# Channel squares of an attention batch from twelve extra loads, and a changed number of unsplit score steps

## The chip, the cores and the metric

The kernel runs on one core of a Trainium2 chip. The metric is the device time of one execution in microseconds (us). Three runs of the kernel before took 2171.54 to 2172.01 us, with a median of 2171.8 us.

## The reference

Four batches (B = 4) of q, k and v with N = 6080 positions and C = 256 channels go through an attention over channels, and its output through a dense layer with a hidden width of 2048:

```python
def _attn_ref(q, k, v, tau):
    qn = q / (np.linalg.norm(q, axis=1, keepdims=True) + 1e-06)
    kn = k / (np.linalg.norm(k, axis=1, keepdims=True) + 1e-06)
    s = kn.transpose(0, 2, 1) @ qn / tau
    s = s - s.max(-1, keepdims=True)
    a = np.exp(s)
    a /= a.sum(-1, keepdims=True) + 1e-09
    return (v @ a).astype(np.float32)

def _moe_ref(x, w_in, w_out):
    h = x @ w_in
    g = h - np.tanh(h)
    return (g @ w_out).astype(np.float32)
```

The norms run over the 6080 positions, one for each channel of q and of k. They are needed before the softmax, but not before the product of k and q, since each is a factor of a row or a column of the scores.

## The kernel before, in words

**Per batch.** The scores are a 256x256 matrix, summed in one PSUM bank over 48 steps of 128 positions (the last has 64). The steps are loaded in groups: group 0 is one step, groups 1 to 23 two steps each, group 24 the tail. From scores and norms comes the softmax matrix e, which is transposed and multiplied into w_in (the "fold", tile `ps_w`, eight pieces of 256 hidden units). The folded weights then meet v in blocks of 2x512 positions by a scheme of seven products (tiles `x`, `y`, `z`), ScalarE (ACT) and VectorE (DVE) form h - tanh(h), and a second product (`ps_o`) gives the output. Six blocks by eight pieces are 48 rounds for each batch, and TensorE (PE) runs them one after another for most of the time.

**Two kinds of score steps.** A plain step (`score`, line 489, with `load_plain`, line 410) multiplies fp32 as it was loaded: two matmuls of 256 columns, which the profile shows as four records. A split step takes a tile `raw`, has ACT write its rounded part and DVE the rest (`split_hi`, `split_lo`, lines 475 and 482), and needs six matmuls in the shorter format. Batch 0 uses 48 plain steps. Batch 1 uses `FILLS` = 48 plain steps, that is all of them, as fillers: the planner puts them on PE where the next instruction of the main line would come late. Batches 2 and 3 use split steps between the rounds.

**Loads at the start.** SyncE (SP) issues every load, in one order, on one queue. A group of q and k is 512 KB (one step 256 KB, the tail 128 KB) and goes into whatever is free at the start: the tiles `vhl` (eight), `gh`/`gl`, `qh`, `ql`; the groups of batch 1 take `qh` and `ql` in turn, two tiles each. Between them stand the pieces of w_in and w_out (`raw_wi`, `raw_wo`, 512 KB each), their converted copies on the way back to memory (`wi_d`), and v (`vraw`, 1 MB).

**Norms of batch 0.** After PE has read a group, ACT squares it in place (`square_plain`, line 424), and DVE and GpSimd (POOL) add the squares of each step, three of four on DVE, to three accumulators (`accumulate`, line 441). At the end ACT copies two of them out of PSUM (`take_squares`), and PE sums over the partitions with matmuls against ones (`sum_squares`, line 451, tile `ps_n`). DVE turns the sums into factors (`add_squares`, `norms`, `scales`), PE spreads one of them (`ps_b`), DVE and ACT make the softmax, PE transposes it (`ps_t`), and the fold starts (`ps_w`). The norms of the other batches come from channel-major loads (`load_channels`, `square`, lines 507 and 516): there a channel is a partition, and ACT's accumulator sums the squares of a row.

**The order of the work.** Nothing is reordered on the chip: a planner (`Plan.order`, line 129) lists all operations ahead of time from costs and due times, and each engine runs its list in order. `plain_load`, `plain_step` and `plain_square` (lines 1059 to 1073) and the loop behind them enter the operations of the first phase.

Of the kernel before, what the change touches and what calls it, by code (L numbers as in the profile page):

```python
# [10 lines left out]
F32 = mybir.dt.float32  # L11
# [3 lines left out]
AF = mybir.ActivationFunctionType  # L15
ALU = mybir.AluOpType
AX = mybir.AxisListType

P = 128
GJ = 2  # L20
NMAX = 512
NSQ = 760
# [13 lines left out]
    ("p6", []), ("p2", [4, "c"]), ("p5", [2]), ("p7", [3, "a", 6]), ("p4", ["d"]), ("p1", [1]), ("p3", [4, "b", 4]),  # L36
]
EARLY = 6
FILLS = 48
FILL_EVERY = 0.6  # L40
LEAD = 6
FIRST = 3
PAD = 208
LAG = 30
# [166 lines left out]
def act_cost(n):  # L211
    return 0.14 + n * 0.0009


def dve_cost(n):
    return 0.157 + n * 0.00104
# [8 lines left out]


@with_exitstack
def attn_moe(ctx: ExitStack, tc: tile.TileContext, qk, v4, qkT, tau, w_in, w_out, outT):

# [3 lines left out]
    nc = tc.nc  # L235
    B, N, _, C = qk.shape
    KC = C // P
# [3 lines left out]
    NJ = N // P  # L241
# [3 lines left out]
    while s0 < N:  # L245
        n = min(NMAX, (N - s0) // 2)
# [10 lines left out]
    g_p = ctx.enter_context(tc.tile_pool(name="g_p", bufs=4))  # L257
# [3 lines left out]
    sm_p = ctx.enter_context(tc.tile_pool(name="sm_p", bufs=1))  # L261
    ps_p = ctx.enter_context(tc.tile_pool(name="ps_p", bufs=1, space=bass.MemoryType.PSUM))
    ring = {
        "wi": Ring(3), "f": Ring(3), "fx": Ring(1), "raw": Ring(3), "qh": Ring(2), "ql": Ring(2), "nt": Ring(2),
        "vraw": Ring(1), "vt": Ring(1), "vhl": Ring(8),
        "u": Ring(3), "c": Ring(4), "t": Ring(4), "gh": Ring(5), "gl": Ring(5), "ob": Ring(2),
    }

    def sb(pool, tag, shape, dtype, name):
        return pool.tile(list(shape), dtype, tag=tag, name=name, bufs=ring[tag].bufs)  # L270

    def bank(i, name, shape=(P, 512)):

        return ps_p.tile(list(shape), F32, tag=f"bank{i}", name=name)
# [6 lines left out]
    def products(out, terms, first, last):  # L281

        seq = []
        for (wh, wl), (xh, xl) in terms:
            seq += [(wh, xh)] if wl is None else [(wh, xl), (wh, xh), (wl, xh)]
        for i, (w, x) in enumerate(seq):
            ins = nc.tensor.matmul(  # L287
                out, w, x,
                start=first and i == 0, stop=last and i == len(seq) - 1,
                skip_group_check=True,  # L290
            )
        return ins
# [63 lines left out]
    wi = {}  # L356
# [30 lines left out]
    groups = []  # L387
    j = 0
    while j < NJ:
        n = min(GJ, NJ - j) if j else NJ % GJ or GJ  # L390
# [7 lines left out]
    class Attn:  # L398
# [117 lines left out]
        def square(self, i):  # L516
# [3 lines left out]
            row, part = divmod(i, N // NSQ)  # L520
            nc.scalar.activation(x, x, AF.Square, accum_out=self.squares[:, row, part:part + 1])

        def add_squares(self):
            self.x = sm_p.tile([P, 2 * KC], F32, name="x")
            if self.acc is None:
                nc.vector.tensor_reduce(self.x, self.squares, axis=AX.X, op=ALU.add)
                nc.vector.tensor_scalar(self.x, self.x, 1e-37, None, op0=ALU.max)
            else:
                nc.vector.tensor_scalar(self.x, self.pn[:, 0:2 * KC], 1e-37, None, op0=ALU.max)

        def norms(self):

# [74 lines left out]


        def fold(self, s, i):
            w = wi.pop((self.b, s))  # L610
            pw = self.pw[s] = bank(i, f"ps_w_{self.b}_{s}", (P, KC, FB))
            for m in range(KC):
                ms = slice(m * P, (m + 1) * P)
                products(
                    pw[:, m, :],
                    [((self.eh[:, kk, ms], self.el[:, kk, ms]), (w[:, 0, kk, :], w[:, 1, kk, :])) for kk in range(KC)],
                    first=m == 0, last=m == KC - 1,
                )
# [79 lines left out]
    plan = Plan()  # L698
# [66 lines left out]
    def banks(gs):  # L765

        return {"X": 2 * (gs % 2), "Y": 1, "Z": 2 - 2 * (gs % 2)}
# [175 lines left out]
    ats = {}  # L943
    beside = {}

    def task(gs, place, what):
        beside.setdefault((gs, place), []).append(what)

    for s in range(FIRST, NS2):
        task(s - 2, "a", lambda s=s: plan_fold(0, s, banks(s - 2)["Z"]))  # L950
# [11 lines left out]
    def plan_softmax(a, sq, ps):  # L962

        r, d, rq, e, total = Buf("r"), Buf("d"), Buf("rq"), Buf("se"), Buf("rs")
        a.ebuf = Buf("e")

        def norms():
            plan.add("DVE", 0.4, a.add_squares, reads=[sq], writes=[r])
            plan.add("DVE", 1.8, a.norms, writes=[r])
            plan.add("DVE", 0.6, a.scales, reads=[r], writes=[d])  # L970

        def spread(z):
            pb = Buf(z)
            plan.add("PE", 0.25, lambda: a.spread(z), reads=[d], writes=[pb], late=0.0 if a.b else 1.0)
            plan.add("ACT", act_cost(C), a.take_spread, reads=[pb], writes=[rq])

        def softmax():
            for m in range(KC):
                plan.add("DVE", 1.1, lambda m=m: a.scaled(m), reads=[ps, rq, r], writes=[e])
                plan.add("ACT", act_cost(C) + 0.1, lambda m=m: a.exp(m), writes=[e])  # L980
            plan.add("DVE", 0.3, a.shares, reads=[e], writes=[total])

        def transpose(z):
            pt = Buf(z)
            plan.add("PE", 0.5, lambda: a.transpose(z), reads=[e], writes=[pt], late=0.0 if a.b else 1.0)
            plan.add("ACT", act_cost(KC * C), a.take_hi, reads=[pt, total], writes=[a.ebuf])
            plan.add("DVE", dve_cost(KC * C), a.take_lo, reads=[pt], writes=[a.ebuf], port=False)

        return norms, spread, softmax, transpose
# [65 lines left out]
    held = {}  # L1055

    scored = []

    def plain_load(b, g):
        at_ = tags[g % len(tags)] if b == 0 else tags[-2 + g % 2]  # L1060
        held[b, g] = [Buf(ring[t[1]]) for t in at_]
        plan.add(
            "SP", 0.35 * len(at_), lambda: ats[b].load_plain(g, at_), writes=held[b, g], size=0.26 * groups[g][1], after=scored if b else (), due=None if b or g > 0 else -20.0 + g,
        )

    def plain_step(b, i, due=None):
# [6 lines left out]
    def plain_square(g):  # L1073
        nonlocal adds
        x = held[0, g]
        if g == 0:
            plan.add("ACT", act_cost(1024), lambda: ats[0].square_plain(g), reads=x, writes=acc)
        else:
            plan.add("ACT", act_cost(1024), lambda: ats[0].square_plain(g), writes=x)
            for j in range(groups[g][1]):  # L1080
                i = adds % 4
                adds += 1
                if i < 3:
                    plan.add(
                        "DVE", dve_cost(2 * C), lambda i=i % 2, j=j: ats[0].accumulate(nc.vector, g, j, i),
                        reads=x, writes=[acc[i % 2]], port=False,
                    )
                else:
                    plan.add(
                        "POOL", pool_cost(2 * C), lambda j=j: ats[0].accumulate(nc.gpsimd, g, j, 2), reads=x, writes=[acc[2]],  # L1090
                    )

    tau_b = Buf("tau_sb")
    plan.add("SP", 0.35, lambda: nc.sync.dma_start(tau_sb, tau), writes=[tau_b], due=0.0)
    for i, (g, jj) in enumerate(steps):
        if jj == 0 and g in early:
            plan_w_in(early[g], due=plan.pe_time, tag="wi" if early[g] < FIRST else "f")
        if i == len(steps) - LEAD:
            scored.append(plan.last_pe)
        plain_step(0, i)  # L1100
        if jj == groups[g][1] - 1:
            plain_square(g)
        if i == 8:
            pt = Buf(1)
            plan.add("PE", 0.1, spread_tau, reads=[tau_b], writes=[pt])
            plan.add("DVE", 0.2, take_tau, reads=[pt], port=False)
    after_scores = plan.pe_time

    fills = [plain_step(1, i, after_scores + FILL_EVERY * i) for i in range(FILLS)]

    sq, pn = [Buf(ring["u"]) for _ in range(2)], Buf(1)
    for x in range(2):
        plan.add("ACT", act_cost(GJ * C), lambda x=x: ats[0].take_squares(x), reads=acc[x:x + 1], writes=sq[x:x + 1])
    plan_moving(0, scored)
    plan.add("PE", 12 * 0.22, lambda: ats[0].sum_squares(1), reads=sq + acc[2:], writes=[pn], late=1.0)
    norms, spread, softmax, transpose = plan_softmax(ats[0], pn, scores[0])
    norms()
    spread(2)
# [6 lines left out]
    for s in range(NS2):  # L1125
        plan_convert(convert_w_out(s), wobuf[s], due=after_scores + 10.0 * s, alone=s > 0)
    for s in range(FIRST, NS2):
        task(max(s - 4, 0), "start", lambda s=s: plan_w_in(s, after=[plan.last_pe], alone=True) if s > EARLY else plan_load_w(0, s))
    for b in range(1, B):
# [3 lines left out]

        plan_scores(b, [(g0 + x0, x) for x0 in range(NS2 + 1 if b == 1 else first, SLOTS - 6) for x in "ab"], ps, FILLS if b == 1 else 0)
        plan_ends(b, plan_channels(b, g0 + first, g0 + SLOTS - 12), ps)
# [21 lines left out]
    for gs in range(TOTAL):  # L1157
# [3 lines left out]
        for name, then in ORDER:  # L1161
# [6 lines left out]
            for x in then:  # L1168
                if isinstance(x, int):
                    lag, x = max(0, lag - x), max(0, x - lag)  # L1170
# [48 lines left out]
```

## Time and profile before

| | |
|---|---|
| median of three runs | 2171.8 us |
| the profiled execution's own time | 2172.18 us |
| its span | 2170.4 us |
| PE busy | 2160.2 us, 10042 matmuls |
| PE weight loads busy | 1817.4 us |
| DVE busy | 1751.0 us |
| ACT busy | 1528.9 us |
| POOL busy | 37.5 us |
| moved by DMA | 342.23 MB |

The span runs from the first instruction to the end of the last one, and the execution's own time is 1.8 us more than it. Busy time is a share of the whole span, so it says little about the first 100 us, in which other work is done than later. A matmul's end is modelled, so PE counts as busy from a matmul's start to a modelled end that overlaps the next one's start; the pace of the work is read from the distance of starts.

### The profile page before, as it was taken

The page shows a single profiled execution, that of the slowest core. Times are in us where ns is not written, and L with a number is a line of the kernel's source. Part 1 is how long each engine was busy: PE and PEld are TensorE (multiplying, and loading weights), DVE is VectorE, ACT ScalarE, POOL GpSimd, SP SyncE. Part 2 cuts the span into 40 slices and gives each one's busy share as a digit, 9 for nine tenths or more (in the row PEclk, how much of TensorE's full clock was granted, in tenths as well). Part 3 has the DMA queues.
Part 4 walks back from the last instruction along what each step waited for, and adds up shares of the span by engine and source line. Part 5 has one row for each costly group of instructions (what it writes and reads, how often), then busy time and mean ns, then how long its engine had stood idle before and what let it go on. Part 6 is the DMA issues. An engine that isn't in the chain of part 4 may idle for free.

```text
span 2170.4 us, 28453 instructions
## 1 busy us (share of the span) xinstructions
PE 2160.2 (100%) x10042; PEld 1817.4 (84%) x10042; DVE 1751.0 (81%) x2842; ACT 1528.9 (70%) x2755; POOL 37.5 (2%) x33
## 2 busy tenths in 40 slices
PE   8999999999999999999999999999999999999999
PEld 7888888888888888888888888888888888888887
DVE  8889877888888777778788877877878878778776
ACT  6566778776777777776677767777667766666665
POOL 5100000000000000000000000000000000000000
PEclk9999999999999999999999999999999999999999
DMA  9944444443454444543345445354333342332331
GB/s 385 346 162 147 163 168 148 161 155 105 151 209 150 172 164 168 181 160 140 126 144 188 170 162 189 143 189 166 128 134 128 122 147 89 128 130 92 125 120 53
DMA packets 82783, 342.23 MB, mean 158 GB/s; under 512 B 9042, under 2 KB 13138, under 8 KB 80082
## 3 DMA queue, kind: packets, MB, share of 16 engines
q1 hardware_dynamic: 82642, 340.43, 43.1%
q8 instruction: 79, 1.29, 0.2%
q14 instruction: 62, 0.51, 0.1%
HBM read 281.94 MB, written 58.46 MB: 157 GB/s over the span
## 4 chain that ended last, share of the span: by engine, by line
PE 97%; DMA 3%; SPq 0%; issue 0%; DVE 0%; ACT 0%
PE ps_o L903 48%; PE x L287 24%; PE y L287 12%; PE z L287 6%; PE ps_s L287 5%; PE ps_w L287 2%; DMA gh<-qk_dram 1%; DMA ql<-qk_dram 1%; DMA vhl<-qk_dram 0%; DMA qh<-qk_dram 0%; DMA raw_wi<-w_in_dram 0%; PE ps_n L456 0%; PE ps_t L598 0%; PE ps_b L563 0%; SPq L464 0%
## 5 line engine op out<-in xcount | busy, mean ns | idle before, releaser
L287 PE MATMUL x<-v,f 128*128 128x512 f32 (+1 forms) x2304 | 613.9, 388 | 0.0
L903 PE MATMUL ps_o<-gh,wo_h 128*128 128x512 f32 (+1 forms) x1536 | 596.8, 389 | 0.0
L903 PE MATMUL ps_o<-gh,wo_l 128*128 128x512 f32 (+1 forms) x1536 | 596.3, 388 | 0.0
L843 DVE TENSOR_TENSOR gl<-t,gh 128x512 fp32r<-128x512 f32 (+1 forms) x768 | 512.4, 680 | 57.7 <-ACT gh L839 55.7
L839 ACT CAST gh<-t 128x512 fp32r<-128x512 f32 (+1 forms) x768 | 463.5, 617 | 68.4 <-DVE t L835 61.1
L287 PEld LDWEIGHTS x<-v,f 128*128 128x128 f32 x2304 | 432.5, 188 | 87.2
L903 PE MATMUL ps_o<-gl,wo_h 128*128 128x512 f32 (+1 forms) x1536 | 472.5, 388 | 0.0
L831 ACT ACTIVATE t<-c 128x512 f32<-128x512 f32 (+1 forms) x576 | 361.1, 627 | 132.6 <-DVE c L819 127.7
L835 DVE TENSOR_TENSOR t<-c,t 128x512 f32<-128x512 f32 (+1 forms) x576 | 392.0, 682 | 75.4 <-ACT t L831 67.8
L803 ACT COPY u<-x 128x512 f32<-128x512 f32 (+1 forms) x384 | 223.6, 582 | 238.5 <-PE x L287 237.4
L903 PEld LDWEIGHTS ps_o<-gh,wo_l 128*128 128x128 f32 x1536 | 288.6, 188 | 56.5 <-ACT gh L839 0.3
L903 PEld LDWEIGHTS ps_o<-gl,wo_h 128*128 128x128 f32 x1536 | 288.6, 188 | 55.3
L903 PEld LDWEIGHTS ps_o<-gh,wo_h 128*128 128x128 f32 x1536 | 288.7, 188 | 53.2
L819 DVE TENSOR_TENSOR c<-u,y 128x512 f32<-128x512 f32 (+1 forms) x384 | 260.7, 679 | 83.7 <-ACT u L803 50.1
L287 PE MATMUL y<-v,f 128*128 128x512 f32 (+1 forms) x1152 | 321.9, 388 | 0.0
L287 PEld LDWEIGHTS y<-v,f 128*128 128x128 f32 x1152 | 216.2, 188 | 43.3 <-DVE t L835 0.3
L831 ACT ACTIVATE t<-x 128x512 f32<-128x512 f32 (+1 forms) x192 | 113.7, 592 | 114.4 <-PE x L287 112.7
L835 DVE TENSOR_TENSOR t<-x,t 128x512 f32<-128x512 f32 (+1 forms) x192 | 131.3, 684 | 72.1 <-ACT t L831 70.4
L819 DVE TENSOR_TENSOR c<-p,z 128x512 f32<-128x512 f32 (+1 forms) x192 | 130.7, 681 | 69.9 <-PE z L287 65.8
L287 PE MATMUL z<-v,f 128*128 128x512 f32 (+1 forms) x576 | 161.2, 388 | 0.0
L287 PEld LDWEIGHTS z<-v,f 128*128 128x128 f32 x576 | 108.1, 188 | 21.5
L803 ACT COPY p<-x 128x512 f32<-128x512 f32 (+1 forms) x192 | 111.8, 582 | 9.6 <-PE x L287 6.7
(121 smaller groups left out, 1494.6 us busy)
## 6 DMA issues: line engine op xcount, KB each, us to landing
f<-f_d SPq DMA_DIRECT2D x160, 896.0 KB, 4.6
nt<-qkT_dram SPq DMA_DIRECT2D x96, 380.0 KB, 5.7
f_d<-f SPq DMA_DIRECT2D x32, 896.0 KB, 3.8
raw<-qk_dram SPq DMA_DIRECT2D x46, 512.0 KB, 5.5
vraw<-v_dram SPq DMA_DIRECT2D x20, 1024.0 KB, 7.8
outT_dram<-ob SPq DMA_DIRECT2D x80, 256.0 KB, 3.0
wi<-wi_d SPq DMA_DIRECT2D x28, 512.0 KB, 5.4
vhl<-qk_dram SPq DMA_DIRECT2D x14, 512.0 KB, 9.8
```

Source lines behind the costliest of these rows:

```text
L287: ins = nc.tensor.matmul(out, w, x, start=first and i == 0, stop=last and i == len(seq) - 1, skip_group_check=True,)
L803: nc.scalar.copy(self.tiles[to], self.tiles["X"][:, 0:self.n])
L819: nc.vector.tensor_add(self.tiles[i], self.tiles[u], self.tiles[ps][:, 0:self.n])
L831: nc.scalar.activation(self.tiles["t", i], self.tiles[c][:, 0:n], AF.Tanh)
L835: nc.vector.tensor_sub(x, self.tiles[c][:, 0:n], x)
L839: nc.scalar.copy(self.g[i][0], self.tiles["t", i])
L843: nc.vector.tensor_sub(self.g[i][1], self.tiles["t", i], self.g[i][0].bitcast(F32))
L903: nc.tensor.matmul(outs[key + (m,)][:, 0:n], (wo_l if part else wo_h)[:, f, m * P:(m + 1) * P], quad.g[i][x], start=first and j == 0, stop ...
```

## The change

Twelve loads are added (`load_early`): the squares of the last twelve full steps of batch 0 (groups 18 to 23) are no longer made by squaring and adding the plain tiles. Instead the host passes those positions of q and k once more, channel-major (`qkE`), in 12 pieces of 128 channels by 512 positions (256 KB each). ACT squares each with its accumulator (`square_early`), DVE adds the three sums of a channel (`add_early`), and `add_squares` adds that to the sums of the other 36 steps. `FILLS` goes from 48 to 43, so that groups 22 to 24 of batch 1 (five steps) become split steps among the rounds. The second group's load has a due time that puts it ahead of the first piece of w_in.

```diff
-FILLS = 48
+FILLS = 43
+LO = 34
+CM = 12
...
+        def load_early(self, i):
+            row, part = divmod(i, CM * P // NMAX)
+            self.channels[i] = sb(g_p, "c", [P, NMAX], F32, f"c_{self.b}_{i}")
+            nc.sync.dma_start(
+                self.channels[i], qkE[row // KC, row % KC * P:(row % KC + 1) * P, part * NMAX:(part + 1) * NMAX],
+            )
+        def square_early(self, i):
...
+            nc.scalar.activation(x, x, AF.Square, accum_out=self.squares[:, row, part:part + 1])
+        def add_early(self):
+            self.x = sm_p.tile([P, 2 * KC], F32, name="x")
+            nc.vector.tensor_reduce(self.x, self.squares[:, :, 0:CM * P // NMAX], axis=AX.X, op=ALU.add)
         def add_squares(self):
...
             else:
-                nc.vector.tensor_scalar(self.x, self.pn[:, 0:2 * KC], 1e-37, None, op0=ALU.max)
+                nc.vector.tensor_add(self.x, self.pn[:, 0:2 * KC], self.x)
+            nc.vector.tensor_scalar(self.x, self.x, 1e-37, None, op0=ALU.max)
...
-            "SP", 0.35 * len(at_), lambda: ats[b].load_plain(g, at_), ..., due=None if b or g > 0 else -20.0 + g,
+            "SP", 0.35 * len(at_), lambda: ats[b].load_plain(g, at_), ..., due=None if b or g > 1 else -20.0 + g,
...
-        if jj == groups[g][1] - 1:
+        if jj == groups[g][1] - 1 and not NJ - CM <= groups[g][0] < NJ:
             plain_square(g)
+        if LO <= i < LO + early_squares:
+            c = Buf(ring["c"])
+            n = i - LO
+            plan.add("SP", 0.35, lambda n=n: ats[0].load_early(n), writes=[c], size=0.26, due=plan.pe_time)
+            plan.add("ACT", act_cost(NMAX) + 0.1, lambda n=n: ats[0].square_early(n), reads=[c], writes=[cm])
...
     plan.add("PE", 12 * 0.22, lambda: ats[0].sum_squares(1), reads=sq + acc[2:], writes=[pn], late=1.0)
+    plan.add("DVE", 0.25, ats[0].add_early, reads=[cm], writes=[cm])
```

On SP, at the loads of the last groups of batch 0 (`vhl_0_18` to `vhl_0_24`), the list before is this; the numbers in a name are batch and group, and a last one that only counts tiles:

```order
L464 DMA vhl_0_18_325<-qk_dram 128x1024
L464 DMA vhl_0_19_332<-qk_dram 128x1024
L464 DMA vhl_0_20_341<-qk_dram 128x1024
L464 DMA vhl_0_21_348<-qk_dram 128x1024
L375 DMA wi_d3_99<-w_3_189 128x1024
L464 DMA vhl_0_22_364<-qk_dram 128x1024
L464 DMA vhl_0_23_372<-qk_dram 128x1024
L467 DMA vhl_0_24_379<-qk_dram 64x512
L322 DMA raw_wo0_387<-w_out_dram 128x1024
L322 DMA raw_wo1_395<-w_out_dram 128x1024
L464 DMA qh_1_0_411<-qk_dram 128x512
```

The same place in the change, from the seventh of the twelve new loads (`c_0_6`) on:

```order
L529 DMA c_0_6_370<-qkE_dram 128x512
L466 DMA vhl_0_20_376<-qk_dram 128x1024
L529 DMA c_0_7_381<-qkE_dram 128x512
L466 DMA vhl_0_21_384<-qk_dram 128x1024
L377 DMA wi_d3_99<-w_3_184 128x1024
L529 DMA c_0_8_401<-qkE_dram 128x512
L466 DMA vhl_0_22_405<-qk_dram 128x1024
L529 DMA c_0_9_413<-qkE_dram 128x512
L529 DMA c_0_10_420<-qkE_dram 128x512
L469 DMA vhl_0_24_425<-qk_dram 64x512
L466 DMA vhl_0_23_431<-qk_dram 128x1024
L529 DMA c_0_11_436<-qkE_dram 128x512
```

Eleven of the twelve new loads now stand ahead of the last load of batch 0, and all twelve ahead of the first load of batch 1; the piece `raw_wo1` has moved behind the loads of batch 1's group 6.

On PE, ahead of the first fold (`ps_w_0_0`), the list before has these filler steps around the transpose (`ps_t`); a full group is four matmuls here, a step two:

```order
L287 MATMUL ps_s_1_448<-ql_1_9_554 128x256 x4
L598 MATMUL ps_t_0_610<-ident_82,s_567 128x128 x4
L287 MATMUL ps_s_1_448<-qh_1_10_573 128x256 x4
L287 MATMUL ps_s_1_448<-ql_1_11_593 128x256 x4
L287 MATMUL ps_s_1_448<-qh_1_12_602 128x256 x2
L287 MATMUL ps_w_0_0_649<-wi_0_0_109,eh_620 128x256 x2
```

And in the change:

```order
L289 MATMUL ps_s_1_472<-qh_1_8_560 128x256 x4
L289 MATMUL ps_s_1_472<-ql_1_9_585 128x256 x2
L619 MATMUL ps_t_0_637<-ident_82,s_591 128x128 x4
L289 MATMUL ps_s_1_472<-ql_1_9_585 128x256 x2
L289 MATMUL ps_s_1_472<-qh_1_10_598 128x256 x4
L289 MATMUL ps_w_0_0_659<-wi_0_0_111,eh_647 128x256 x2
```

The fold stood behind 24 filler steps, and stands behind 21 of them now; 24 of 48 were left behind it before, and 22 of 43 are now.

On SP, the first five loads before:

```order
L464 DMA vhl_0_0_106<-qk_dram 128x512
L322 DMA raw_wi0_108<-w_in_dram 128x1024
L1094 DMA tau_sb_89<-tau_dram 1x1
L464 DMA vhl_0_1_112<-qk_dram 128x1024
L322 DMA raw_wi1_114<-w_in_dram 128x1024
```

And in the change:

```order
L466 DMA vhl_0_0_106<-qk_dram 128x512
L466 DMA vhl_0_1_108<-qk_dram 128x1024
L324 DMA raw_wi0_110<-w_in_dram 128x1024
L1117 DMA tau_sb_89<-tau_dram 1x1
L324 DMA raw_wi1_114<-w_in_dram 128x1024
```

Group 1 and the first piece of w_in have changed places; what follows is the same.

## Rows read from the trace of the kernel before

**Rows 1.** The page: span, and DMA share in 40 slices of 54 us.

```profile
span 2170.4 us, 28453 instructions
...
DMA  9944444443454444543345445354333342332331
```

**Rows 2.** Waits of PE over the whole span: us in total, times, longest.

```profile
PE ps_s L287 <- DMA vhl<-qk_dram: 5.9, 3, 3.5
PE ps_s L287 <- DMA ql<-qk_dram: 0.3, 1, 0.3
```

**Rows 3.** Chain that ended last, first 85 us: start us, us, what.

```profile
2.41 6.63 DMA raw_wi<-w_in_dram
...
9.05 9.40 DMA gh<-qk_dram
...
43.55 9.22 DMA ql<-qk_dram
...
62.66 6.07 DMA ql<-qk_dram
```

**Rows 4.** Windows: engines' busy us, granted clock, DMA share, GB/s.

```profile
10.00:20.00 10.00, 10.00 (x44) 8.44 (x43) 7.74 (x15) 6.39 (x8) 4.18 (x3) 1.00 1.03 416
20.00:30.00 10.00, 10.00 (x48) 8.80 (x47) 9.47 (x14) 8.32 (x13) 8.23 (x6) 1.00 1.04 413
30.00:40.00 10.00, 9.84 (x46) 8.31 (x45) 8.72 (x15) 7.51 (x10) 7.13 (x6) 1.00 1.03 420
40.00:50.00 10.00, 10.00 (x47) 8.79 (x47) 9.69 (x15) 6.71 (x8) 6.41 (x6) 1.00 1.03 383
50.00:60.00 10.00, 9.76 (x53) 7.94 (x52) 9.76 (x18) 4.48 (x7) 4.04 (x4) 0.95 1.03 422
...
70.00:80.00 10.00, 10.00 (x54) 8.94 (x53) 8.21 (x18) 2.37 (x7) 0.71 (x1) 1.00 0.87 283
```

**Rows 5.** Timeline of SP's issues: start us, us, what.

```profile
9.05 0.33 SPq L464 DMA_DIRECT2D gh<-qk_dram  x1
10.29 0.33 SPq L464 DMA_DIRECT2D gl<-qk_dram  x1
...
18.47 0.33 SPq L464 DMA_DIRECT2D gh<-qk_dram  x1
19.10 0.33 SPq L464 DMA_DIRECT2D gl<-qk_dram  x1
...
38.58 0.56 SPq L467 DMA_DIRECT2D vhl<-qk_dram  x1
```

**Rows 6.** DMA issues of the first 80 us: KB each, median us to landing.

```profile
vhl<-qk_dram SPq DMA_DIRECT2D x1, 128.0 KB, 10.1
```

**Rows 7.** Timeline of PE: start us, us, what, idle before and its releaser.

```profile
3.52 2.07 PE L287 MATMUL ps_s<-vhl 128*128 128x256 f32 x4 [3.52 <-DMA vhl<-qk_dram]
7.79 8.86 PE L287 MATMUL ps_s<-vhl 128*128 128x256 f32 x32 [2.20 <-DMA vhl<-qk_dram]
...
23.04 1.03 PE L287 MATMUL ps_s<-gl 128*128 128x256 f32 x4
23.90 1.03 PE L287 MATMUL ps_s<-gh 128*128 128x256 f32 x4
...
51.58 1.13 PE L287 MATMUL ps_s<-qh 128*128 128x256 f32 x4
...
56.37 0.50 PE L456 MATMUL ps_n<-ones,sq 128*128 128x1 f32 x4
...
58.97 3.66 PE L287 MATMUL ps_s<-ql 128*128 128x256 f32 x8
...
78.62 0.59 PE L287 MATMUL ps_w<-wi,eh 128*128 128x256 f32 x2
```

**Rows 8.** Timeline of DVE in the same stretch.

```profile
52.09 3.07 DVE L444 TENSOR_TENSOR acc<-vhl,acc 128x512 f32<-128x512 f32 x5
...
64.10 1.49 DVE L557 TENSOR_SCALAR diag<-ident,r 128x128 f32<-128x128 f32 x2
```

**Rows 9.** Chain at 700 us: a split step of batch 2.

```profile
702.58 0.71 PE ps_s L287 x6
```

**Rows 10.** Windows, as in rows 4: the low clock, and the rounds behind the start.

```profile
58.90:62.40 3.50, 3.50 (x10) 2.50 (x10) 3.20 (x10) 0.87 (x2) 1.27 (x1) 0.52 1.01 373
...
90.00:190.00 100.00, 100.00 (x470) 83.80 (x469) 92.47 (x167) 69.07 (x126) 0.00 (x0) 1.00 0.54 199
```

More of the change, by code (lines that the diff above doesn't have):

```diff
@@ L227, in attn_moe @@
 @with_exitstack
-def attn_moe(ctx: ExitStack, tc: tile.TileContext, qk, v4, qkT, tau, w_in, w_out, outT):
+def attn_moe(ctx: ExitStack, tc: tile.TileContext, qk, v4, qkT, qkE, tau, w_in, w_out, outT):
     nc = tc.nc
@@ L521, in square @@
             nc.scalar.activation(x, x, AF.Square, accum_out=self.squares[:, row, part:part + 1])
+        def load_early(self, i):
[5 more added lines that the diff above has]
+        def square_early(self, i):
+            row, part = divmod(i, CM * P // NMAX)
+            if i == 0:
+                self.squares = sm_p.tile([P, 2 * KC, N // NSQ], F32, name="squares")
+            x = self.channels.pop(i)
+            nc.scalar.activation(x, x, AF.Square, accum_out=self.squares[:, row, part:part + 1])
+        def add_early(self):
+            self.x = sm_p.tile([P, 2 * KC], F32, name="x")
+            nc.vector.tensor_reduce(self.x, self.squares[:, :, 0:CM * P // NMAX], axis=AX.X, op=ALU.add)
         def add_squares(self):
-            self.x = sm_p.tile([P, 2 * KC], F32, name="x")
             if self.acc is None:
+                self.x = sm_p.tile([P, 2 * KC], F32, name="x")
                 nc.vector.tensor_reduce(self.x, self.squares, axis=AX.X, op=ALU.add)
-                nc.vector.tensor_scalar(self.x, self.x, 1e-37, None, op0=ALU.max)
             else:
-                nc.vector.tensor_scalar(self.x, self.pn[:, 0:2 * KC], 1e-37, None, op0=ALU.max)
+                nc.vector.tensor_add(self.x, self.pn[:, 0:2 * KC], self.x)
+            nc.vector.tensor_scalar(self.x, self.x, 1e-37, None, op0=ALU.max)
         def norms(self):
@@ L609, in fold @@
         def fold(self, s, i):
-            w = wi.pop((self.b, s))
+            w = wi[self.b, s]
             pw = self.pw[s] = bank(i, f"ps_w_{self.b}_{s}", (P, KC, FB))
@@ L967, in norms @@
         def norms():
-            plan.add("DVE", 0.4, a.add_squares, reads=[sq], writes=[r])
+            plan.add("DVE", 0.4, a.add_squares, reads=[sq] if a.b else [sq, cm], writes=[r])
             plan.add("DVE", 1.8, a.norms, writes=[r])
@@ L1062, in plain_load @@
         plan.add(
-            "SP", 0.35 * len(at_), lambda: ats[b].load_plain(g, at_), writes=held[b, g], size=0.26 * groups[g][1], after=scored if b else (), due=None if b or g > 0 else -20.0 + g,
+            "SP", 0.35 * len(at_), lambda: ats[b].load_plain(g, at_), writes=held[b, g], size=0.26 * groups[g][1], after=scored if b else (), due=None if b or g > 1 else -20.0 + g,
         )
@@ L1091, in plain_square @@
                     )
+    early_squares = 2 * KC * CM * P // NMAX
+    cm = Buf("cm")
     tau_b = Buf("tau_sb")
@@ L1203 @@
         "qkT_dram": np.ascontiguousarray(np.transpose(np.stack([q, k]), (0, 1, 3, 2))),
+        "qkE_dram": np.ascontiguousarray(
+            np.stack([q[0], k[0]])[:, :N // P * P].reshape(2, P, N // P, C)[:, :, -CM:].transpose(0, 3, 2, 1).reshape(2, C, CM * P)
+        ),
         "tau_dram": np.ascontiguousarray(tau).reshape(1, 1),
```

## The prediction

> **What bounds the kernel now.** I first read the page and the waits of PE. The page shows the DMA engines busy at nine tenths in the first slices and at four tenths later [rows 1]. PE waits for nothing in the whole span but loads of q and k: 5.9 us and 0.3 us, all in the first 70 us [rows 2]. So from there on the time is the sum of PE's work, and only the start has idle time to win or to lose.
>
> The chain of waits tells what sets the start. It runs from load to load: one ends at 9.04 us, the next at 18.45, and so on to the one that starts at 43.55 and lands at 52.77; PE takes over only then, and a load comes in again from 62.66 to 68.73 [rows 3]. The windows agree: from 10 to 60 us the DMA share is 1.03 in every ten microseconds, at 416, 413, 420, 383 and 422 GB/s, a mean of 411 [rows 4]. The queue is full. PE counts as busy beside it, yet has no lead: the first step of batch 1 starts at 51.58 us [rows 7], 2.9 us behind the landing of batch 0's last load (issued at 38.58 [rows 5], landed 10.1 us later [rows 6], thus at 48.7).
>
> So before the fold (78.62 us [rows 7]) the time goes with the bytes that stand in SP's list ahead of what PE needs, and after it with PE's work.
>
> **The change, part by part.** A plain step takes 0.86 us on PE (23.04 to 23.90 [rows 7]), a split step 0.71 us [rows 9].
>
> *The twelve loads.* Each is 256 KB. Loads of 256 KB are issued 0.63 us apart where loads land one by one (18.47 and 19.10), and those behind 512 KB landings 1.24 us apart (9.05 and 10.29) [rows 5]: half the bytes, half the time. Eleven stand ahead of batch 0's last load, 2,816 KB or 2.88 MB, at 411 GB/s 7.0 us. It lands at 48.7 + 7.0 = 55.7 us.
>
> The Trainium skill ("DMA: Bandwidth & Descriptors", sections "Bandwidth" and "Rules for kernel authors") speaks against such loads: it asks for 1 MiB or more, and its table has 341 GB/s for 1 MB and 138 GB/s for 64 KB. By that the twelve loads would take 9.2 to 22.8 us instead of 7.7, and my sum would rise by 1.5 to 15 us (an estimate from that page); the issue times above speak against it, since this queue holds several loads at once.
>
> *To the norms.* The last load is now group 23: the list has the tail ahead of it. PE takes three steps (2.6 us) after it, to 58.3 us. The first three groups of batch 1 stand behind twelve new loads, but without `raw_wo1`: 2,560 KB more, 6.4 us later than before, so the first would start at 58.0 and PE takes it at 58.3. Five steps (4.3 us) bring PE to 62.6 us, where `ps_n` stands; before it was 56.37 [rows 7].
>
> Is `ps_n` ready by then? Before, DVE was the last to be ready: its adds ran in one row of five from 52.09 to 55.16 [rows 8], after PE's last step. Nine of DVE's adds (12 steps, three of four) go, some 0.61 us each in that row, 5.5 us in all; only the tail's square, its add and a copy remain behind PE's last step, about 2 us, so at 60 to 61 us. This shortening is real, but it lies beside the wait for loads and buys nothing. ACT's twelve new squares land in an engine that is busy 6.71 and 4.48 us of ten there [rows 4] and loses six squares of whole groups: no cost. POOL loses three adds: none.
>
> *From the norms to the fold.* `ps_n` takes 2.6 us (56.37 to 58.97 [rows 7]), to 65.2. The DVE work from there to the end of `diag` took 6.6 us before (58.97 to 65.59 [rows 7, 8]); I take 7, because three operations on `raw_wi6` replace one on v, so PE can spread at 72.3 and transpose from about 78. PE itself needs more loads for that: the transpose is now behind the first step of group 9. Summing SP's list, 19,072 KB landed up to the load that ended at 52.77 [rows 3], and 29,824 KB stand in the changed list up to group 9: 10,752 KB more, or 11.01 MB, 26.8 us at 411 GB/s, thus 79.6 us. With its first step (0.86), the transpose (0.4) and three more steps (2.6) the fold starts at 83.5 us instead of 78.62: **+4.9 us**. That the fold needs three filler steps fewer ahead of it is in this.
>
> *After the fold* there were 24 plain steps, 20.6 us. Now there are 22 plain steps (18.9) and five split ones (3.55): **+1.8 us**. The whole saving of five splits, 0.75 us, is inside it. The splits' ACT and DVE work lies beside PE, as for the 96 split steps of batches 2 and 3, in which PE waits for nothing [rows 2].
>
> *Group 1 ahead of w_in.* PE waited 2.20 us for it at 7.79 [rows 7]. That is at most what the step can win, and at least nothing. I take nothing: group 2 stands behind the same bytes as before, and whatever lead PE has is used up where it meets the queue, before the last loads of batch 0.
>
> **Sum:** +4.9 + 1.8 = **+6.7 us**. The profiled execution took 2172.18 us, 0.4 more than the median, so I predict 2171.8 + 6.7 = 2178.5 us. The bounds: at 422 GB/s, the fastest window, group 9 lands 0.7 us sooner, at 383 GB/s 1.9 us later [rows 4]. Below that, 2.2 us if the lead at the start is kept. Above, 1.7 us for two fillers that no longer cover a wait where DVE is busy 92% of the time (90 to 190 us [rows 10]), and 1.7 us for a stretch at the low clock (below). The forecast alone spans 2176 to 2182.
>
> **The rivals.**
>
> *A longer stall through the clock.* At the start PE ran four matmuls in 2.07 us that later take 1.03, and from 58.90 to 62.40, right behind the 24 tiny matmuls of `ps_n`, the granted clock was 0.52, the 1.2 GHz level nearly throughout; eight matmuls took 3.66 us [rows 7, 10]. In the change PE idles in many small pieces between 30 and 58 us. One more such stretch costs 1.75 us (half of 3.5), two 3.5, where they do not lie in a wait: 2180 to 2182 us. Against it, the small waits before did not lower the clock. The Trainium skill ("TensorE: Matmul & The Clock Gate", "HAM oscillation — how this bites in real kernels") says that waits for DMA between bursts of matmuls bring the clock down; here the trace shows a fall only behind `ps_n`.
>
> *The loads are absorbed, and DVE's tail was the bound (faster).* If the queue takes the twelve loads without making batch 0's last load later than about 49 us, what counts is DVE's tail: `ps_n` no longer trails PE's last step by 4.8 us (51.58 to 56.37 [rows 7]), and the fold is ready three filler steps (2.6 us) earlier. With 2.2 us at the start and 0.75 us from the splits that gives -5.5 us, 2166.3. For it speaks DVE's 9.7 busy us of ten [rows 4]; against it the DMA share of 1.03.
>
> *Half of it is absorbed (no change).* SP's list also has lulls before: from 70 to 80 us the share is 0.87 at 283 GB/s [rows 4]. If the new loads only push others into those lulls, and the 2.2 us of the start are kept, +6.7 - 2.2 - 1.5 leaves 3 us, 2174.8.
>
> *The step that does nothing.* Group 1 ahead would be one, and is counted as nothing already.
>
> **How the numbers follow.** A measurement of this kernel can tell about 0.2%, 4.3 us. Forecast 0.58, clock 0.17, half absorbed 0.18, absorbed 0.07. Forecast and clock lie above 2176.1, so slower 0.74 (a hundredth goes to the middle), same 0.19, faster 0.07. The range of 2174.5 to 2182.5 us takes in the forecast with its bounds, most of the clock's case and half of the middle one, and leaves out the faster case.
>
> **What would show it.** In the profile after: waits of PE for `vhl`, some 10 us or more instead of 5.9; batch 0's last load landing near 55.7 us; `ps_n` at about 62.6 and the first `ps_w` at about 83.5 us; a DMA share of 1.03 up to 80 us; `ps_s` of batch 1 as groups of six among the rounds. If the last `vhl` load lands before 50 us, or PE starts the fold before 79 us, the forecast is wrong. If the fold starts at 83 us and the time is still the same, then the rounds behind it hid a wait that I could not see.

## The result and the profile after

The changed kernel takes 2178.44 us (median of 7 runs, 2178.11 to 2179.03), the kernel before 2172.01 us beside it (7 runs, 2171.54 to 2173.22): a ratio of 1.0029 (95% interval 1.0020 to 1.0038), **6.4 us or 0.3% slower**. The profiled execution took 2178.13 us.

The page, to be held against [rows 1]:

```profile
span 2176.4 us, 28513 instructions
...
DMA  9944454443354544544345445354333342332331
```

The span is 6.0 us longer. The waits of PE over the whole span (us in total, times, longest):

```profile
PE ps_s L289 <- DMA vhl<-qk_dram: 10.3, 7, 3.6
PE ps_s L289 <- DMA ql<-qk_dram: 3.6, 4, 1.4
```

They sum to 13.9 us, against 6.2 us before [rows 2]. That is 7.7 us more. Of these 1.7 us are given back, since the stretch at the low clock behind `ps_n` (3.5 us at 0.52 [rows 10]) did not occur in this execution, and 0.75 us by the five split steps, by the prediction's prices. That leaves some 5.3 us, and PE's last product starts 5.4 us later than before; the rest of the 6.0 us comes behind it. So the loss comes from the waits of the start, and none of it is a new wait in the rounds: PE still waits for loads alone.

The windows of the start (columns as in [rows 4]):

```profile
40.00:50.00 10.00, 7.71 (x34) 5.75 (x32) 7.89 (x13) 5.82 (x13) 5.00 (x5) 1.00 1.03 413
50.00:60.00 10.00, 7.44 (x32) 5.41 (x31) 2.58 (x6) 4.61 (x12) 2.10 (x2) 1.00 1.04 400
60.00:70.00 10.00, 8.62 (x52) 7.58 (x50) 5.16 (x21) 2.80 (x6) 2.53 (x2) 1.00 1.02 415
70.00:80.00 10.00, 9.16 (x44) 7.52 (x45) 8.69 (x18) 5.81 (x13) 3.46 (x2) 1.00 1.03 420
```

The DMA share stays above 1.0 up to 80 us, where it had been 0.87 from 70 us on. DVE, which was busy 9.7 us of ten from 40 to 60 us, falls to 7.89 and then 2.58: the adds are gone, and nothing got faster by it. PE falls as well, to 7.71 and 7.44.

The chain that ended last, from 40 us (start us, us, what):

```profile
40.01 7.06 DMA c<-qkE_dram
...
47.15 7.73 DMA vhl<-qk_dram
...
54.92 7.57 PE ps_s L289 x32
```

One of the new loads now stands in the chain, and the last load of batch 0 lands at 54.88 us. PE's timeline there:

```profile
20.09 1.03 PE L289 MATMUL ps_s<-gh 128*128 128x256 f32 x4
...
54.92 3.05 PE L289 MATMUL ps_s<-vhl 128*128 128x256 f32 x12 [1.38 <-DMA vhl<-qk_dram]
57.91 1.13 PE L289 MATMUL ps_s<-qh 128*128 128x256 f32 x4
62.33 0.50 PE L458 MATMUL ps_n<-ones,sq 128*128 128x1 f32 x4
64.92 1.97 PE L289 MATMUL ps_s<-ql 128*128 128x256 f32 x8
79.66 0.60 PE L619 MATMUL ps_t<-ident,s 128*128 128x128 f32 x4
82.50 0.59 PE L289 MATMUL ps_w<-wi,eh 128*128 128x256 f32 x2
```

The same step of `gh` in the kernel before, the first behind the eight `vhl`:

```profile
22.17 1.03 PE L287 MATMUL ps_s<-gh 128*128 128x256 f32 x4
```

So at 20 us PE is 2.1 us ahead: group 1's early load is worth there about the 2.2 us that PE had waited for it before [rows 7]. By 57.91 it is 6.3 us behind (51.58 [rows 7]), and the fold starts 3.9 us late with three filler steps (2.6 us) fewer ahead of it.

DVE in the same stretch:

```profile
56.34 0.17 DVE L542 TENSOR_REDUCE x<-squares 128x4 f32<-128x12 f32 x1 [8.11 <-ACT c L538]
...
65.10 0.16 DVE L549 TENSOR_TENSOR x<-ps_n,x 128x4 f32<-128x4 f32 x1 [4.32 <-PE ps_n L458]
69.20 0.47 DVE L578 TENSOR_SCALAR diag<-ident,r 128x128 f32<-128x128 f32 x2
```

It waited 8.11 us for the new squares, and was 4.32 us idle before the sums: no longer late, but waiting for what comes late on other engines.

### The profile page after: what moved, and what is told of

Same layout as the page of the kernel before. It is cut to its first block, busy times and chain, and to the rows that moved or that the text cites. A ratio compares the mean times of both kernels' runs of the same rounds, so it can differ in the third digit from the quotient of the medians.

```text
span 2176.4 us, 28513 instructions
## 1 busy us (share of the span) xinstructions
PE 2158.1 (99%) x10052; PEld 1813.9 (83%) x10052; DVE 1749.2 (80%) x2838; ACT 1533.5 (70%) x2776; POOL 33.7 (2%) x30
## 4 chain that ended last, share of the span: by engine, by line
PE 97%; DMA 3%; SPq 0%; ACT 0%; issue 0%; DVE 0%
PE ps_o L924 48%; PE x L289 24%; PE y L289 12%; PE z L289 6%; PE ps_s L289 5%; PE ps_w L289 2%; DMA ql<-qk_dram 1%; DMA vhl<-qk_dram 1%; DMA gl<-qk_dram 1%; DMA c<-qkE_dram 0%; PE ps_n L458 0%; SPq L466 0%; PE ps_t L619 0%; PE ps_b L584 0%; SPq L324 0%
```

## The experiments

Times are medians; ratios are against the kernel before, measured beside them (2172.2 to 2172.5 us).

### One part of the change alone: e1_first and e2_fills43

`e1_first` is the kernel before with group 1 ahead.

```diff
-... due=None if b or g > 0 else -20.0 + g,
+... due=None if b or g > 1 else -20.0 + g,
```

> The kernel before, with group 1 ahead of the first piece of w_in and nothing else changed in the program text. Queue theory (time before the fold follows the bytes in SP's list): PE's wait of 2.2 us before group 1 shrinks to about 1.3 us, PE leads by about 2 us up to 35 us, and gives it back in waits for loads by the last groups of batch 0; time 2171.0 to 2172.5 us, within 0.8 us of before. Rival (the lead at the start is kept): 2169.6 us.

Measured: 2173.06 us, 1.0004 (0.9995 to 1.0012). No gain, as the prediction had it, but not for the reason it gave. PE's timeline at the first step of batch 1 and at `ps_n`:

```profile
50.13 1.13 PE L287 MATMUL ps_s<-qh 128*128 128x256 f32 x4
...
57.51 0.61 PE L456 MATMUL ps_n<-ones,sq 128*128 128x1 f32 x4 [0.98 <-ACT sq L448]
```

At 50.13 us a lead of 1.45 us is still there (51.58 before [rows 7]): the queue has not used it up. It goes behind that. The planner orders what follows a little otherwise and puts two more filler steps ahead of `ps_n` (1.7 us), PE has a new wait of 1.0 us for ACT's copy `sq`, the profiled execution spends 6.8 us at the low clock where the kernel before spent 3.4 (1.7 us more lost), and in the rounds PE waits 0.8 us for ACT and DVE. That execution, at 2174.91 us, is the slowest of eleven; the fastest took 2170.84 us.

`e2_fills43` is the kernel before with five steps split.

```diff
-FILLS = 48
+FILLS = 43
```

A lookup in `fold` no longer deletes its entry besides, as in the changed kernel; no instruction comes of that.

> The kernel before with 43 plain steps of batch 1 and five split ones; the first 100 us of every list stay as they were. Queue theory: only PE's work changes, five steps by 0.86 - 0.71 us, so -0.75 us: 2170.8 to 2171.6 us. Rival (the split steps or the missing fillers are what costs in the change): slower than 2172.5 us.

Measured: 2174.53 us, 1.0010 (1.0001 to 1.0019): 2.3 us slower, where a gain of 0.75 was expected. **A miss that told most.** PE waits in the rounds, which the kernel before never does:

```profile
PE x L287 <- DVE v L695: 0.6, 1, 0.6
PE y L287 <- DVE c L819: 0.4, 1, 0.4
PE z L287 <- DVE t L835: 0.3, 1, 0.3
PE ps_o L903 <- DVE gl L843: 0.2, 1, 0.2
```

All lie between 184 and 190 us. The window there (columns as in [rows 10]) has DVE busy 24.77 of 25 us:

```profile
170.00:195.00 25.00, 23.52 (x100) 18.03 (x99) 24.77 (x42) 17.13 (x34) 0.00 (x0) 1.00 0.35 123
```

In the kernel before the last fillers stood in that place. The first pair of products `x` behind them, before:

```profile
193.83 1.53 PE L287 MATMUL x<-v,f 128*128 128x512 f32 x6
```

The same pair in `e2_fills43`:

```profile
192.22 1.52 PE L287 MATMUL x<-v,f 128*128 128x512 f32 x6
```

Five plain steps fewer stand ahead of it, 4.3 us by their pace, and it comes only 1.6 us sooner (its fold started 0.6 us later, at 79.18 us); the five split steps (3.55 us) come on top later. So the rounds up to some 195 us do not go at PE's pace by themselves: the plain steps fill what the other engines, DVE by its busy time, leave open.

### The loads alone: e3_insert and e3_tiny

The kernel before, its lists kept, with twelve loads like those of the change put ahead of groups 16 to 24. Nothing reads them. `e3_tiny` loads 64 of the 512 positions.

```diff
+AHEAD = {16: (0, 1), 17: (2, 3), 19: (4,), 20: (5, 6), 21: (7,), 22: (8,), 23: (9, 10), 24: (11,)}
+COLS = 512      # e3_tiny: 64
...
         for op in plan.order():
+            for n in loads.get(op, ()):
+                ats[0].load_early(n)
             op.run()
```

> The kernel before with the twelve 256 KB loads alone, put into SP's list at the places that they have in the change; nobody reads them, and the lists of all other engines are unchanged. Queue theory: batch 0's last load lands 7.5 us later (near 56 us), the first fold starts 4 to 5.5 us later (near 83 us), time 2175.8 to 2177.5 us. Rival (the loads are absorbed, and the moved and removed steps cost the time): 2171 to 2173 us.

> As the run with the twelve loads alone, but each of 64 columns, a row of 256 bytes: as many loads at the same places with an eighth of the bytes. Queue theory with bytes as the price: 0.9 us of queue time, time 2171.8 to 2173.0 us. Rival (each load costs as such, through its issue or its place among those in flight): 2175.5 us or more.

Measured: 2179.44 us, 1.0035 (1.0022 to 1.0047), and 2174.94 us, 1.0011 (1.0002 to 1.0020). Both were expected too low. The first sum of norms on PE's timeline, in `e3_insert`:

```profile
63.91 0.50 PE L459 MATMUL ps_n<-ones,sq 128*128 128x1 f32 x4
```

And in `e3_tiny`:

```profile
57.76 0.50 PE L459 MATMUL ps_n<-ones,sq 128*128 128x1 f32 x4
```

It was 56.37 before [rows 7]. Twelve loads of 256 KB cost 7.5 us there, 0.63 us each, or 3.15 MB at 417 GB/s: the bytes alone are enough for the whole loss at that place. Twelve loads with an eighth of the bytes cost 1.4 us, where an eighth would be 0.9. How far single profiles agree is seen in `e2_fills43`, in which SP issues the same loads in the same order up to 60 us and `ps_n` still starts 1.0 us later than before (57.38 us). So 7.5 us is clear of that, and the half microsecond between 1.4 and 0.9 is not. The profiled execution of `e3_insert` (2181.39 us, the slowest of its five) also spends 6.8 us at the low clock behind `ps_n`, where the kernel before spent 3.4, which costs 1.7 us more; some of the 7.2 us may be that.

### The bytes taken out of the change: e4_small, e5_unread, e6_store

If bytes are enough, taking them away should give the time back. `e4_small` is the changed kernel with 64 positions in each new load and square; the squares of the others are left out of batch 0's norms.

```diff
-                self.channels[i], qkE[..., part * NMAX:(part + 1) * NMAX],
+                self.channels[i][:, 0:64], qkE[..., part * NMAX:part * NMAX + 64],
...
-            x = self.channels.pop(i)
+            x = self.channels.pop(i)[:, 0:64]
```

> The changed kernel with each of the twelve channel-major loads, and the ACT square on it, cut to 64 of its 512 positions; every engine's list is that of the change. The squares of the other 448 positions of those pieces are left out of batch 0's norms. Theory (the bytes ahead in the queue are the cost): 2,688 KB less are moved, 6.5 us at 422 GB/s; but twelve small loads of the same kind cost 2.7 us when they stood alone in the list of the kernel before. So batch 0's last load lands by 50 to 51 us, ps_n starts at 57 to 59 us, PE waits for vhl 4 to 7 us, and the median is 2172 to 2175 us; as DVE's tail is shorter here than in that earlier run and group 1 is ahead, I take 2173.5. Rival (the cost is in the changed lists of PE, DVE and SP, not in the bytes): ps_n stays at 62 us and the time at 2177.5 to 2179 us.

Measured: 2177.79 us, 1.0026 (1.0017 to 1.0036). **The rival's time: most of the loss stays,** 5.4 of 6.4 us, each against the kernel before beside it. The rival put it down to the changed lists of PE, DVE and SP. The trace tells which list; the queue is now far from full (windows as above):

```profile
40.00:50.00 10.00, 8.56 (x40) 7.15 (x39) 8.79 (x14) 3.17 (x12) 4.93 (x4) 1.00 0.84 280
50.00:60.00 10.00, 6.95 (x28) 4.64 (x27) 3.33 (x7) 3.46 (x12) 4.06 (x4) 1.00 0.86 294
```

PE waits for loads while the DMA engines have room, so the loads must be issued late. SP's waits from 30 to 55 us (us in total, times, longest):

```profile
SPq L529 <- ACT c L538: 6.6, 5, 2.4
SPq L377 <- POOL w L356: 2.8, 2, 2.5
```

And SP's timeline (start us, us, what):

```profile
37.03 0.38 SPq L466 DMA_DIRECT2D vhl<-qk_dram  x1
39.51 0.33 SPq L529 DMA_DIRECT2D c<-qkE_dram  x1
39.93 0.38 SPq L466 DMA_DIRECT2D vhl<-qk_dram  x1
42.94 0.33 SPq L377 DMA_DIRECT2D wi_d<-w  x1
...
46.49 0.50 SPq L466 DMA_DIRECT2D vhl<-qk_dram  x1
49.49 0.33 SPq L529 DMA_DIRECT2D c<-qkE_dram  x1
```

SP issues in order. The load at 39.51 needs a tile `c` that ACT has not squared yet, the store at 42.94 a piece of w_in that POOL has not converted, the load at 49.49 a tile `c` again; each holds back the loads of q and k behind it, some 2.5 us at a time. The last `vhl` is issued at 46.49 us, hardly before the 47.15 us of the full loads. It lands sooner, and PE takes it at 51.59 us instead of 54.92; but the first load of batch 1 stands behind the third hold and is issued at 50.78 us (50.49 in the changed kernel), and PE waits for it and the next two. The Trainium skill ("DMA: Bandwidth & Descriptors", "Anatomy of one DMA — SWDGE (gpsimd) path"), in a section on transfers that GpSimd issues, says that DMA engines do not wait on semaphores and that the issuing sequencer does so before it dispatches; these rows, of transfers that SP issues, agree.

In the changed kernel itself, with the full loads, the waits for `c` are shorter (SP's waits in the same stretch):

```profile
SPq L529 <- ACT c L538: 2.5, 5, 0.7
```

The store waits for nothing but landings there. So with the full loads it is the landings that come last, and the holds take over once the bytes are gone. The hold at the store is not even new: in the kernel before SP waits 2.2 us for POOL at the same store, beside a full queue.

Two runs take the holds away one after the other. `e5_unread` squares a constant tile, so that a `c` is free when its load has landed; `e6_store` moves the store behind batch 0's last load besides. Both leave the squares of the last twelve full steps out of the norms.

```diff
-            nc.scalar.activation(x, x, AF.Square, ...)
+            nc.scalar.activation(self.scratch, ones[:, 0:64], AF.Square, ...)
```

```diff
-        for op in plan.order():
+        ops = list(plan.order())
+        ops.remove(kept[3])
+        ops.insert(ops.index(loads[23]) + 1, kept[3])
+        for op in ops:
```

> The run before (e4_small: twelve loads of 64 positions each, lists of the change) with ACT's twelve squares made of a constant tile instead of the loaded ones, so that a c tile is free when its load has landed; all other instructions and their order stay. The squares of the last twelve full steps are left out of batch 0's norms. Theory (in e4_small the bytes were gone, but SP, which issues in order, was held 6.6 us by c tiles that ACT had not yet squared, at 37 to 39.5 us and at 47 to 49.5 us, and 3.3 us by the w_in stores that wait for POOL): the first hold goes, and the second; batch 1's first load is issued at 47 to 48.5 us instead of 50.8, ps_n starts at 58.5 to 60 us instead of 61.4, and the median is 2174.5 to 2176.5 us. Rival (the holds of SP are short of what the queue has in flight, PE's waits have another cause): 2177.3 to 2178.5 us.

> The run e5_unread with one more edit: the store of the fourth converted w_in piece (wi_d3), which waits for POOL in front of batch 0's last three loads, stands behind them. The squares of the last twelve full steps are left out of batch 0's norms. Theory (the hold of SP at that store is the rest of the delay): batch 0's last load is issued 2 to 3 us sooner than in e5_unread, ps_n at 56.5 to 58.5 us, 2172.5 to 2174.5 us. Rival: as e5_unread, within 0.7 us.

Measured: 2175.84 us, 1.0016 (1.0007 to 1.0024), and 2173.56 us, 1.0007 (0.9998 to 1.0016). Both fell where the theory of the holds put them. The first fold on PE's timeline in `e4_small`:

```profile
82.23 0.58 PE L289 MATMUL ps_w<-wi,eh 128*128 128x256 f32 x2
```

The same line in `e5_unread`:

```profile
80.30 0.58 PE L289 MATMUL ps_w<-wi,eh 128*128 128x256 f32 x2
```

And in `e6_store`:

```profile
78.60 0.59 PE L289 MATMUL ps_w<-wi,eh 128*128 128x256 f32 x2
```

The spans (2175.8, 2174.1 and 2172.2 us) follow these starts step by step. In `e5_unread` the store alone now holds SP, from 38.72 to 43.24 us on its timeline:

```profile
38.72 0.33 SPq L466 DMA_DIRECT2D vhl<-qk_dram  x1
43.24 0.33 SPq L377 DMA_DIRECT2D wi_d<-w  x1
...
46.58 0.52 SPq L466 DMA_DIRECT2D vhl<-qk_dram  x1
```

In `e6_store` the last `vhl` goes out 2.7 us sooner, ahead of the store (SP's timeline):

```profile
43.87 0.34 SPq L466 DMA_DIRECT2D vhl<-qk_dram  x1
44.30 0.38 SPq L377 DMA_DIRECT2D wi_d<-w  x1
```

So two limits lie close together at the start: bytes in the queue, which set the time of the changed kernel, and SP held by tiles that other engines must free, which sets it when the bytes are gone. Either one makes most of the loss alone (7.2 us in `e3_insert`; 5.4 us in `e4_small`, of which taking away the two holds wins 4.2), and together they make 6.4. `e5_unread` also frees ACT of its waits for the small loads; what that wins by itself is not separated. What is left in `e6_store`, 1.1 us, is within what the measurement can tell, but the traces place it: the fold, with three filler steps fewer ahead of it, starts where it did before (78.60 and 78.62 us), and from there to the first fold of batch 1 PE takes 501.7 us instead of 499.9. That is the prediction's +1.8 us for 22 plain and five split steps instead of 24 plain ones.

### Splits put back, and versions that might beat both

`a_fills48` is the changed kernel with `FILLS = 48`.

> The changed kernel with FILLS back at 48, so that the last five steps of batch 1 stay plain fillers; up to the fold and some 100 us behind it the lists are those of the change. Theory of the prediction (a split step saves 0.15 us, the rounds hide the rest): +0.75 us, 2179.2 us. Rival (as the kernel before with FILLS 43 showed, the plain fillers cover waits at 175 to 191 us and five splits cost as much as five plain steps): 2176.2 to 2178.0 us, with PE waits for v, c and t gone or smaller.

Measured: 2179.63 us, 1.0034 (1.0021 to 1.0046), 7.2 us above the kernel before, against 6.4 of the changed kernel. So the rival falls: PE waits for nothing from 80 to 400 us in either. The two intervals overlap, and this profile has a low-clock stretch (1.7 us lost) that the other lacks, so the times do not show the saving of 0.75 us. The traces have most of it: from the first fold to that of batch 1 PE takes 0.5 us more than in the changed kernel (502.2 and 501.7 us).

`i1_keep` is the changed kernel with the stores of w_in's first pieces later, `i2_keep` the kernel before with that and with group 1 first.

```diff
+KEEP = 40.0
-... reads=[w], size=0.52, due=plan.pe_time)
+... reads=[w], size=0.52, due=plan.pe_time + (KEEP if s < EARLY else 0.0))
```

> The changed kernel with the stores of the converted w_in pieces due 40 us later for the first six pieces, so that they leave the queue of the first 60 us: 19,328 KB instead of 21,632 stand up to the first load of batch 1. Theory (bytes in the queue): 2,304 KB less, 5.7 us at 411 GB/s: ps_n at 57 to 58 us, the fold at 77 to 79 us, PE waits for vhl 4 to 6 us instead of 10.3, and 2172.5 to 2174.5 us, since the stores find room behind 80 us where the DMA share is 0.61. Rival (the loads are not what holds the fold, or the stores hold up w_in's or v's loads later): over 2177 us.

> The kernel before (no extra loads, FILLS 48) with group 1 ahead of the first piece of w_in and the same later stores: 17,536 KB up to the first load of batch 1 instead of 19,072, 3.8 us at 411 GB/s. Theory (bytes in the queue): PE's 6.2 us of waits for loads shrink by 2 to 4 us, the first step of batch 1 starts at 48 to 49.5 us, and the time is 2168.5 to 2170.5 us, faster than both kernels. Rival (with the queue shorter DVE's tail ahead of ps_n is the bound, as the 4.8 us from batch 1's first step to ps_n suggest; PE fills it with steps that are plain anyway, so no loss but a later wait for fillers): 2171 to 2173 us with new waits of PE for sq or for v.

Measured: `i1_keep` 2176.50 us, 1.0017 (1.0009 to 1.0026), with times from 2174.07 to 2179.43; `i2_keep` 2174.58 us, 1.0011 (1.0002 to 1.0020). Both missed. In `i1_keep` PE waits 3.11 us for the last `vhl`, up to 50.05 us, and the clock falls (windows):

```profile
50.00:60.00 10.00, 9.95 (x23) 7.16 (x24) 8.20 (x12) 4.27 (x9) 4.63 (x5) 0.52 1.01 403
60.00:70.00 10.00, 10.00 (x52) 8.78 (x51) 5.42 (x19) 4.41 (x9) 2.41 (x2) 0.83 0.93 320
```

A grant of 0.52 over ten microseconds is 4.8 us of full clock lost: the prediction's rival of the clock, in another kernel. The 0.83 behind it (1.7 us) is a second stretch, right behind `ps_n`, as in the kernel before. This execution, at 2178.58 us, is one of the slower ones of its kernel, so the median need not hold all of that. The Trainium skill ("TensorE: Matmul & The Clock Gate", "HAM oscillation — how this bites in real kernels"), which the prediction weighed, says that waits for DMA between bursts of matmuls bring the clock down; this trace agrees. In the profiled execution of the changed kernel, whose single waits between 30 and 76 us are 1.8 us or less, no fall is seen.

`i2_keep` got what it was built for: in its chain PE runs from 14.6 to 54.1 us without a break, and the fold starts at 73.05 us, 5.6 us sooner than before [rows 7]. It gives that back, and more, at 165 to 195 us. The waits of PE from 100 to 200 us:

```profile
PE ps_o L904 <- ACT gh L840: 1.2, 1, 1.2
PE x L288 <- DVE v L696: 1.2, 1, 1.2
PE z L288 <- DVE t L836: 0.8, 1, 0.8
```

And the window at their end (columns as in [rows 10]):

```profile
170.00:200.00 30.00, 27.46 (x107) 20.05 (x106) 29.79 (x52) 20.43 (x38) 0.00 (x0) 0.94 0.34 111
```

DVE is busy 29.79 of 30 us, all fillers are used up by then, and the clock falls once more (0.94). It looks like `e2_fills43` again: a PE that comes sooner meets DVE. The stores that now stand behind 80 us differ as well; what they cost is not separated.

`j1_cm8` (the changed kernel with `CM = 8`, `FILLS = 48` and the later stores) and `j2_pool` (`i2_keep` with more adds on POOL) try to lessen both limits.

```diff
-CM = 12
+CM = 8
```

```diff
-                i = adds % 4
-                if i < 3:
+                i = adds % 8
+                if i not in (2, 5, 7):
```

> The changed kernel with eight loads instead of twelve (the squares of eight full steps of batch 0 made from them, those of the others as before), the w_in stores 40 us later and FILLS 48: 18,048 KB up to the first load of batch 1, against 19,072 in the kernel before and 17,536 in i2_keep. Theory (the time at 195 us is set by PE's idle time at the start or by DVE's work up to there, whichever is more; this version lessens both, DVE by six adds or 3.7 us): 2169.0 to 2171.0 us, no PE waits for v, c or gh at 165 to 195 us. Rival (the clock falls behind a wait of the start, 1.7 to 3.4 us, or SP is held by the c tiles as in e4_small): 2172.5 to 2175 us.

> i2_keep (group 1 first, later w_in stores, no extra loads) with three of eight adds of squares on POOL instead of two: DVE has six adds less, some 3.7 us, POOL six more of 1.3 us. Theory (i2_keep started its fold 5.6 us sooner than the kernel before but lost it at 165 to 195 us, where DVE sets the pace and no fillers were left): 2170.0 to 2172.5 us, the waits of 165 to 195 us down from 3.6 to under 2 us. Rival (DVE's work ahead of 80 us is not what the rounds wait for, or POOL slows DVE): 2173.5 to 2176 us.

Measured: `j1_cm8` 2173.64 us, 1.0007 (0.9998 to 1.0016), `j2_pool` 2180.21 us, 1.0037 (1.0025 to 1.0050). In `j1_cm8` the rounds wait for nothing, as its theory had it, but PE waits 6.0 us for `vhl`, SP is held 3.4 us by tiles `c`, and 6.8 us at the low clock cost 3.4 us (half of them behind `ps_n`, as in the kernel before): its rival. In `j2_pool` the list moved too: POOL stood idle 12.1 us for ACT's rounded part of a w_in piece, the fold came at 77.81 us, and PE waited 3.3 us for `qh` behind it. What fewer adds on DVE are worth by themselves it does not tell. No version beat the kernel before.

## Why the prediction was right, and where its reasons were not

It said +6.7 us, 2178.5; measured were +6.4, 2178.44.

- **Last load of batch 0** at 55.7 us: 54.88. **First step of batch 1** at 58.3: 57.91. **`ps_n`** at 62.6: 62.33, its operands ready at 60.4 (ACT's last copy ends there), as the 60 to 61 of the text. DVE's shorter tail was real and bought nothing, since PE was later still.
- **Fold** at 83.5: 82.50. PE took the first step of group 9 at 78.69 us instead of 79.6 (the loads of 60 to 80 us went at 415 and 420 GB/s instead of 411), and what stands behind it took as long as forecast: a term of +3.9 instead of +4.9. The piece from the end of the sums to the end of `diag` took 4.75 us (64.92 to 69.67) instead of 7, but was not on the path: ACT had `s` ready at 76.3 us, 3.4 us before PE transposed it.
- **After the fold** +1.8: the last product of the trace starts at 2171.64 instead of 2166.21 us, 5.4 us late, of which 3.9 were there at the fold: +1.5. Up to the first fold of batch 1 (584.2 us instead of 578.5) it was +1.8, just as forecast. Another 0.5 us came behind that last product, where the trace shows the output's end alone; it varies by as much between kernels (4.2 to 4.8 us from there to the end of the span), and nothing here explains it.
- **Group 1** counted as nothing: a lead of 2.1 us at 20 us, used up between 30 and 38 us, where PE waits for `ql` and `vhl` (0.19 us at 30.80, 1.24 at 35.76, 0.53 at 38.28). That is right for the change, but the queue alone does not do it: without the new loads 1.45 us of lead outlive batch 0's last load (`e1_first`).
- **Clock:** no fall at the start of the profiled execution. The experiments' profiles spend from none to 13.7 us of their first 85 us at the low level (`e3_tiny`, `i1_keep`), so this is a term of 0 to 6.8 us that differs between kernels and executions.
- **Range of the forecast:** the bounds listed add up to 2175.6 and 2183.8 us; the 2176 to 2182 of the text leaves part of them out without a word.

Two of its reasons hold in the changed kernel, but less far than they were written. "The queue is full", so the time "goes with the bytes": `e4_small` took 2.75 MB (12 x 448 of 512 positions) away and brought the loss from 6.4 us to 5.4 only. The step that falls short is the one that counted only the bytes of the twelve loads and never asked what tile each needs, who frees it, and what is queued on SP behind it. It did the number no harm because with full loads the bytes come last; that they do was not worked out, and so far it was luck. And "from there on the time is the sum of PE's work" holds only as long as the fold comes no sooner and the fillers last: `e2_fills43` and `i2_keep` show a second limit close below, up to about 195 us, where PE waits for DVE's and ACT's results once the plain fillers are missing. That DVE sets the pace there is read from its busy share and from the releasers; no run took DVE's work away there by itself. It makes the faster rival (2166.3 us) unlikely even with the loads absorbed; no run shows that case.

The rule of the Trainium skill ("DMA: Bandwidth & Descriptors", "Rules for kernel authors") on loads of 1 MiB or more did not hold here: by an estimate from that page's table the prediction weighed the twelve at 9.2 to 22.8 us, and `e3_insert` shows 7.5 us.

## What to carry to other kernels

Where one engine issues all transfers in order, a new load costs its bytes and can also bring a hold: look for the tile it goes into, the engine that frees it, and what is queued behind. When two limits lie close together, taking one away shows little (1.0 of 6.4 us here); take them away one after the other before calling either harmless. And work that fills gaps costs less than its own length where it covers another engine's pace: taking five plain steps (4.3 us) away from the last place of the fillers saved 2.2 us there in `e2_fills43`.

## What the runs showed of the hardware

- 256 KB loads, queued many at a time, cost 0.63 us each (417 GB/s, `e3_insert`); loads of an eighth of that, with rows of 256 bytes, cost 1.4 us for twelve (`e3_tiny`), where their bytes alone would be 0.9 us, a difference within the 1.0 us by which single profiles differ at that place.
- SP issues in order: in `e4_small` and `e5_unread` a load or store whose tile is not free holds those behind it for 2.4 to 3.3 us at a time, with a DMA share of 0.83 to 0.86 around them.
- After the 24 one-column matmuls of `ps_n` the granted clock fell to the 1.2 GHz level in some profiled executions and not in others (before, `e2_fills43`, `a_fills48`, `i1_keep`, `j1_cm8` and `j2_pool`: 3.4 us; `e1_first` and `e3_insert`: 6.8 us; after, `e3_tiny`, `e4_small`, `e5_unread`, `e6_store` and `i2_keep`: none). In `e1_first` PE had waited 1.0 us ahead of them; in the kernel before it had not. What decides it stays open.
